# Regrouping a retention-and-adapters kernel so that two units share each TensorE array mode

## Chip, core and metric

The kernel runs on one core of a Trainium2 chip. The core has five engines that run side by side, each with its own queue of instructions in a fixed order: TensorE (PE in the profile; its weight loads are listed as PEld), VectorE (DVE), ScalarE (ACT), GpSimd (POOL) and SyncE (SP, which here only issues DMA transfers). They wait for each other through semaphores. TensorE writes only into PSUM, eight banks of 128 partitions by 2 KB; DVE and ACT read it from there. The metric is the time of one execution on the device in microseconds (us).

## What is computed

The first half is a retention layer: attention without softmax, with a causal mask that decays with the distance. The second half is a mixture of small low-rank adapters, of which each token uses its best two.

```python
# q, k, v: (B=8, H=8, S=576, D=64)
scores = q @ k.T / sqrt(D)
gamma  = 1 - 2.0 ** (-5 - arange(H))
Dmat   = where(i >= j, gamma ** (i - j), 0)
x      = (scores * Dmat) @ v              # then (B*S, H*D) = (4608, 512)

logits = x @ w_gate                       # 8 experts
topk   = two largest logits; w = softmax over these two
out    = x + sum over the two of  w * (x @ A[e]) @ B[e]     # rank 16
```

## The kernel before

**Tiling.** The 576 positions are four chunks of 128 and one of 64. A *quad* is one chunk of four batches (half of the eight), so there are ten quads; `quads` lists them, chunk by chunk. A *unit* is two batches of a quad: `units` has 16 full units (0 to 15) and two half units (16 and 17) for the last, 64 long chunk. Inside a chunk the products are computed directly with a mask; what comes from the earlier chunks is held in a decayed state `P`, one per pair of batches.

**Stages.** Each unit t passes these functions. The third column is the part of TensorE's array that its matmuls use, as the profile prints it (rows*columns): its *array mode*. The half units use 64*64 for S and R.

| stage | TensorE work | mode | what follows on other engines |
|---|---|---|---|
| `stage_T` | transposes q, k to `pqT`, `pkT` | 64*128 | copies to `qT`, `kT` by ACT (some by DVE) |
| `stage_S` | scores `ps` = kT . qT (half units: `pe`) | 64*128 | DVE multiplies by the mask into `rt` (`rh`) |
| `stage_Q` | `px` = state P . qT | 64*64 | nothing; no matmuls for units 0 to 3 |
| `stage_U` | `pu` = k . v, the state's update | 128*64 | DVE adds P into `pn`, POOL decays it into `P` |
| `stage_R` | `px` += v . rt | 128*64 | DVE scales it into `xT` |
| `stage_Z` | `pz` = xT . (A, gate) | 128*128 | DVE: `lg`, two largest, `ns` |
| `stage_V` | none | | ACT: two sigmoids `sg` |
| `stage_W` | none | | DVE: weights `cm`, weighted `zc`; frees `pz` |
| `stage_B` | transposes xT into `po` | 64*128 | nothing |
| `stage_X` | transposes zc into `pzt` | 128*128 | ACT copies it to `zT` |
| `stage_Y` | `po` += zT . B | 128*128 | ACT copies `po` to `osb` (half of it by DVE where `spread`), SP issues the output |

`scale_k` lets POOL multiply k by the decay in place, after k's transposition and before U.

**What sets the order.** The helpers `mm`, `vec` and `act` (lines 80 to 87) chain all instructions of TensorE, DVE and ACT in the order in which the stages are called, so the calls at the end of the kernel are the engines' queues. PSUM is handed out by `bank` and `done` (lines 102 to 110): `free` is a list, first in, first out; a bank that is given back goes to its end, and the next user waits for its last reader. The loads are issued by `issue(n)` for quad n + 2 when quad n begins; DMA issues stand on SP's queue, so one that waits for a free buffer holds the ones behind it, outputs too. The pool `io` holds three buffers each for q, k and v of a quad.

**The order before.** Unit 0 and 1 are written out by hand with the setup. Unit t in the steady part runs

```python
stage_S(t, (0,)); stage_V(t - 1); stage_T(t + 1, ("qT",))
stage_S(t, (1,)); stage_W(t - 1); stage_T(t + 1, ("kT",))
stage_B(t - 1); stage_Q(t); stage_U(t); scale_k(t + 1)
stage_R(t); stage_X(t - 1); stage_Z(t); stage_Y(t - 1)
```

so each unit's T is one unit ahead and its B, X, W and Y one unit behind. At unit 15, `stage_Q(16)` is called as well. The half units have an order of their own, and the last unit ends half by half (`gs`).

Of the kernel before, what the change touches and what calls it, by code (L numbers as in the profile page):

```python
# [10 lines left out]
FP32 = mybir.dt.float32  # L11
# [7 lines left out]
def kernel(  # L19
# [180 lines left out]
    def issue(n):  # L200
        if n >= len(quads):
            return
        c, qd = quads[n]
        first = n == 0
        tl = [
            iop.tile([128, QUAD, H, Dh], FP32, tag=tag, name=tag) for tag in ("q32", "k32", "v32")
        ]
        if c == NFULL:
            if qd > 0:
                return  # L210
            for src, dst in zip((q, k, v), tl):
# [40 lines left out]
    def is_full(t):  # L252
        return units[t][0] < NFULL
# [11 lines left out]
                op=ALU.mult,  # L265
            )

    def stage_T(t, names=("qT", "kT")):

        s = st.setdefault(t, {})  # L270
        for nm in names:
            src = nat[units[t]][0 if nm == "qT" else 1]
            dst = s[nm] = wk.tile([128, 2, HP, C], FP32, tag=nm, name=nm)
            ps = [bank([128, HP, 2, L], f"p{nm}") for _ in range(2)]
            for hp in range(HP):
                for b in range(2):
                    for g in range(2):
                        mm(
                            ps[g][:, hp, b, :],
                            lhsT=src[rows(g), b, 2 * hp : 2 * hp + 2, :],  # L280
                            rhs=id64[rows(g), :],
                            is_transpose=True,
                            start=True,
                            stop=True,
                        )
            for g in range(2):
                if is_full(t):
                    o = dst[:, :, :, rows(g)].rearrange("p b a i -> p a b i")
                else:
                    o = dst[:, g].rearrange("p a (b i) -> p a b i", b=2)  # L290
                if t < 2 and nm == "qT" or t < 3 and nm == "kT" and g == 1:
                    vec("tensor_copy", out=o, in_=ps[g])
                else:
                    act("copy", out=o, in_=ps[g])
            done(*ps)

    def stage_Q(t):
        c, qd, sl = units[t]
        s = st[t]
        s["px"] = px = [  # L300
            bank([128, HP, C], f"px{x}") for x in range(2)
        ]
# [94 lines left out]
    def stage_R(t):  # L397
# [5 lines left out]
        if is_full(t):  # L403
            for b in range(2):
                for hp in range(HP):
                    for ho in range(2):
# [9 lines left out]
                xt = mo.tile([128, HP, C], FP32, tag="xT", name="xT", bufs=6)  # L416
                vec("tensor_tensor", out=xt, in0=px[b], in1=asc[b], op=ALU.mult)
                s["xT"].append(xt)
            done(*px)
# [11 lines left out]
                            skip_group_check=True,  # L431
                        )
        for x in range(2):
            xt = mo.tile([128, HP, C], FP32, tag="xT", name="xT", bufs=6)
# [26 lines left out]

    BOTH = (0, 1)

    def stage_X(t, gs=BOTH):
        s = st[t]
        n = len(gs)
        pzt = bank([128, n, 128], "pzt", FP16)
        for y, g in enumerate(gs):
            mm(
                pzt[:, y, :], lhsT=s["zc"][g], rhs=ident16,  # L470
                is_transpose=True, start=True, stop=True,
            )
        zt = mo.tile([128, n, 128], FP16, tag=f"zT{n}", name="zT")
        act("copy", out=zt, in_=pzt)
        done(pzt)
        for y, g in enumerate(gs):
            s.setdefault("zT", {})[g] = zt[:, y, :]

    def stage_Z(t, gs=BOTH):
        s = st[t]  # L480
# [38 lines left out]
    def stage_W(t, gs=BOTH):  # L519
# [6 lines left out]
        zc = mo.tile([128, n, ER], FP16, tag=f"zc{n}", name="zc")  # L526
        for y in range(n):
            vec(
                "scalar_tensor_tensor",
# [78 lines left out]
    for t in range(NU):  # L608
        if units[t][2] == 0:
            issue(quads.index(units[t][:2]) + 2)  # L610
        if t == 0:
# [9 lines left out]
            for ho in range(2):  # L621
                gp.tensor_copy(out=AW[1][rows(ho)], in_=AW[0][rows(1 - ho)])
            gp.dma_start(out=Bcat, in_=moe_B.rearrange("e r d -> (e r) d"))
            stage_Q(0)
            stage_U(0)
            stage_R(0)
            stage_T(1, ("qT",))
            stage_T(1, ("kT",))
            scale_k(1)
            stage_Z(0)  # L630
            stage_S(1)
            stage_W(0)
            stage_Q(1)
            stage_U(1)
# [13 lines left out]
            continue  # L648
        if t == 1:
            continue  # L650
        if t == NU - 1:
            break
        if t == 2:
            stage_T(3, ("qT",))
            stage_B(1)
            stage_V(1)
            stage_S(2)
            stage_W(1)
            stage_T(3, ("kT",))
            stage_Q(2)  # L660
            stage_U(2)
            scale_k(3)
            stage_R(2)
            stage_X(1)
            stage_Z(2)
            stage_Y(1)
            continue
        if is_full(t):
            stage_S(t, (0,))
            stage_V(t - 1)  # L670
            stage_T(t + 1, ("qT",))
            stage_S(t, (1,))
            stage_W(t - 1)
            stage_T(t + 1, ("kT",))
            stage_B(t - 1)
            stage_Q(t)
            if not is_full(t + 1):
                stage_Q(t + 1)
            stage_U(t)
            scale_k(t + 1)  # L680
            stage_R(t)
            stage_X(t - 1)
            stage_Z(t)
            stage_Y(t - 1)
            continue

        stage_S(t)
        stage_W(t - 1)
        stage_T(t + 1)
        stage_B(t - 1)  # L690
        stage_R(t)
        stage_Q(t + 1)
        stage_X(t - 1)
        stage_Z(t)
        stage_W(t)
        stage_Y(t - 1)
        stage_S(t + 1)
        stage_B(t)
        stage_X(t)
        stage_R(t + 1)  # L700
        stage_Y(t)
        for g in range(2):
            stage_Z(t + 1, (g,))
            stage_W(t + 1, (g,))
        stage_B(t + 1)
        for g in range(2):
            stage_X(t + 1, (g,))
            stage_Y(t + 1, (g,), spread=True, last=True)
    return

# [1 line left out]
_INS = ['q', 'k', 'v', 'moe_w_gate', 'moe_A', 'moe_B']  # L712
_OUTS = [((4608, 512), 'float32')]
# [25 lines left out]
```

## Time and profile before

| what | value |
|---|---|
| median of 13 runs | 194.59 us (193.70 to 195.32) |
| the profiled execution's own time | 193.94 us |
| its span, first to last instruction | 192.1 us |
| TensorE's granted clock, mean | 0.992 of full speed |
| last po matmul's end, by the timeline | 187.56 us from the span's start |
| DMA | 38.73 MB, mean 202 GB/s |
| a masked product `rt` on DVE (128x512) | 0.686 us, x64 |
| a copy of `qT` or `kT` on ACT (128x512) | 0.590 us |
| k scaled on POOL (128x512) | 1.042 us, x32 |

A row of the timeline has the start and the time of a group in us, the engine, the line (81 for all matmuls, 84 for DVE, 87 for ACT: the helpers), the operation, "out<-in", the array mode for TensorE, the shape and the count. A bracket at its end is idle time of that engine just before, with what ended it. TensorE's matmuls overlap each other and their ends are modelled, so the distance from one start to the next says more than the printed time.

### The profile page before, as it was taken

The numbers are of one execution on the slowest core, as the hardware profiler recorded it, in microseconds if no ns is written. First come the engines' busy times: TensorE is split into PE (matmuls) and PEld (weight loads), VectorE is DVE, ScalarE is ACT, GpSimd is POOL, SyncE is SP. The second block draws the span as 40 slices with busy tenths as digits, with TensorE's granted clock in tenths as the row PEclk, the third lists the DMA queues.
The fourth block names the chain that finished last, engine by engine and source line by source line (L and its number), as shares of the span: only waits on it lengthen the run. The fifth ranks groups of instructions, "written<-read, shape, count | busy, mean of one in ns | idle before, by whom it ended". The sixth has DMA issues, their size and how long they took to land. (4 is left out here: it accounts for less than half of the span.)

```text
span 192.1 us, 8113 instructions
## 1 busy us (share of the span) xinstructions
PE 180.4 (94%) x3612; PEld 163.4 (85%) x3612; DVE 110.4 (57%) x281; ACT 72.0 (37%) x195; POOL 58.9 (31%) x70
## 2 busy tenths in 40 slices
PE   7899997999999999999999999999999999987870
PEld 2499997989999999999999999999999999986750
DVE  4467947574656564747465665646464645543650
ACT  4111163253526160707071615252525344160540
POOL 8994025040424242332414150606060510200000
PEclk9999999999999999999999999999999999999996
DMA  7999699998998999579799758998951102030343
GB/s 143 263 240 269 170 277 271 242 315 227 248 361 263 245 337 273 143 216 332 222 241 312 213 169 250 296 263 206 230 145 50 64 26 90 3 113 3 113 109 109
DMA packets 53746, 38.73 MB, mean 202 GB/s; under 512 B 27472, under 2 KB 49104, under 8 KB 53712
## 3 DMA queue, kind: packets, MB, share of 16 engines
q1 hardware_dynamic: 52736, 37.75, 70.1%
q8 instruction: 28, 0.46, 1.0%
q10 hardware_dynamic: 832, 0.34, 0.7%
q0 software_dynamic: 144, 0.13, 0.4%
q14 instruction: 6, 0.05, 0.1%
HBM read 28.91 MB, written 9.44 MB: 200 GB/s over the span
## 5 line engine op out<-in xcount | busy, mean ns | idle before, releaser
L261 POOL TENSOR_TENSOR k<-k,pack 128x512 f32<-128x512 f32 x32 | 32.7, 1042 | 79.9 <-PE pkT L81 69.3
L84 DVE TENSOR_TENSOR rt<-ps,mask 128x512 f32<-128x512 f32 x64 | 41.0, 686 | 16.5 <-PE ps L81 16.0
L81 PE MATMUL pz<-AW,xT 128*128 128x136 f32 x288 | 37.4, 283 | 0.2 <-DVE xT L84 0.2
L81 PE MATMUL ps<-qT,kT 64*128 64x128 f32 x512 | 35.7, 281 | 0.9 <-DVE kT L84 0.9
L81 PEld LDWEIGHTS pz<-AW,xT 128*128 128x128 f32 x288 | 34.6, 190 | 0.6 <-DVE xT L84 0.5
L81 PEld LDWEIGHTS ps<-qT,kT 64*128 64x128 f32 x512 | 31.0, 188 | 4.0 <-PE po L81 2.7
L87 ACT COPY osb<-po 128x256 f32<-128x256 f32 x68 | 20.6, 386 | 28.4 <-PE po L81 28.0
L81 PE MATMUL px<-rt,v 128*64 128x128 f32 x512 | 30.8, 273 | 0.0
L84 DVE TENSOR_TENSOR xT<-px,asc 128x512 f32<-128x512 f32 x36 | 24.6, 691 | 8.1 <-PE px L81 6.9
L81 PEld LDWEIGHTS px<-rt,v 128*64 128x64 f32 x512 | 27.8, 137 | 0.0
L87 ACT COPY zT<-pzt 128x256 f16<-128x256 f16 (+1 forms) x19 | 6.9, 361 | 53.4 <-PE pzt L81 53.4
L87 ACT COPY kT<-pkT 128x512 f32<-128x512 f32 x33 | 17.9, 590 | 14.2 <-PE pkT L81 14.2
L395 POOL TENSOR_TENSOR P<-pn,gdec 128x512 f32<-128x512 f32 x12 | 15.3, 1271 | 25.5 <-DVE pn L84 22.6
L87 ACT COPY qT<-pqT 128x512 f32<-128x512 f32 x32 | 17.2, 590 | 8.3 <-PE pqT L81 8.3
L81 PE MATMUL pu<-v,k 128*64 128x64 f32 x512 | 18.4, 225 | 1.6 <-POOL k L261 1.1
L81 PEld LDWEIGHTS pu<-v,k 128*64 128x64 f32 x512 | 16.3, 138 | 4.1 <-issue 2.6
L84 DVE COPY lg<-pz 128x16 f32<-128x16 f32 (+1 forms) x19 | 3.3, 173 | 26.6 <-PE pz L81 26.6
L84 DVE TENSOR_TENSOR pn<-pu,P 128x512 f32<-128x512 f32 x12 | 8.3, 692 | 16.0 <-PE pu L81 16.0
L81 PE MATMUL px<-qT,P 64*64 64x128 f32 (+1 forms) x512 | 15.9, 262 | 1.3 <-issue 1.3
L81 PEld LDWEIGHTS px<-qT,P 64*64 64x64 f32 x512 | 12.7, 133 | 2.3 <-issue 1.4
L81 PE MATMUL po<-id,xT 64*128 64x64 f32 x288 | 12.6, 224 | 0.7 <-DVE zc L84 0.7
L81 PE MATMUL pkT<-id,k 64*128 64x64 f32 x288 | 12.4, 223 | 0.1
(51 smaller groups left out, 150.0 us busy)
## 6 DMA issues: line engine op xcount, KB each, us to landing
out_dram<-osb SPq DMA_DIRECT2D x32, 256.0 KB, 3.8
q<-in_q_dram SPq DMA_DIRECT2D x4, 512.0 KB, 6.5
k<-in_k_dram SPq DMA_DIRECT2D x4, 512.0 KB, 6.8
v<-in_v_dram SPq DMA_DIRECT2D x4, 512.0 KB, 7.0
out_dram<-osb SPq DMA_DIRECT2D x6, 128.0 KB, 2.3
Arow<-in_moe_A_dram SPq DMA_DIRECT2D x1, 256.0 KB, 5.0
out_dram<-osb ACTq DMA_DIRECT2D x2, 128.0 KB, 2.7
Bcat<-in_moe_B_dram POOLq DMA_DIRECT2D x1, 128.0 KB, 4.9
```

The lines of the kernel that those rows point to most:

```text
L81: chain("pe", nc.tensor.matmul(*args, **kw))
L84: chain("dve", getattr(nc.vector, fn)(**kw))
L87: chain("act", getattr(nc.scalar, fn)(**kw))
L261: gp.tensor_tensor(out=kk[:, b], in0=kk[:, b], in1=gv[:, 0].unsqueeze(2).broadcast_to((128, H, Dh)), op=ALU.mult,)
L395: nc.gpsimd.tensor_tensor(out=Pt, in0=pn, in1=gdec, op=ALU.mult)
```

## The change

- *Order.* From unit 2 on, the two units of a quad go together through each mode. In the loop at an even t from 4 to 14, with u = t, t + 1: S of both, with the T of units t + 2 and t + 3 between their halves; B of units t - 4 and t - 3, one common X for both; Z of t - 2, Y of t - 4 and t - 3, Z of t - 1; Q of both; W of t - 2 and t - 1 (DVE alone); U and R of t, then of t + 1. So T runs a quad ahead, Z and W a quad behind, and B, X, Y two quads behind. The quad of units 4 and 5 has its own T at the end of the start and issues T of 6 and 7 at its end.
- *Start.* Units 2 and 3, T of 4 and 5 move into the part written out by hand; V(1) stands ahead of Y(0). U comes before Q in units 0 to 3, so that U gets the first bank of the free list. The copy of unit 0's kT is cut into one per batch (two on ACT, two on DVE).
- *Tail.* S(16) and Q(16) follow R(15), then the remaining stages of units 12 to 17.
- *Buffers.* q: two instead of three; qT: four instead of two; zc: four instead of three; zT: two instead of three; xT: eight instead of six. k, v and kT stay at three, three and two.

```diff
@@ issue
-            iop.tile([128, QUAD, H, Dh], FP32, tag=tag, name=tag) for tag in ("q32", "k32", "v32")
+            iop.tile([128, QUAD, H, Dh], FP32, tag=tag, name=tag, bufs=n)
+            for tag, n in (("q32", 2), ("k32", 3), ("v32", 3))
@@ stage_T
-    def stage_T(t, names=("qT", "kT")):
+    def stage_T(t, names=("qT", "kT"), shared=False):
-            dst = s[nm] = wk.tile([128, 2, HP, C], FP32, tag=nm, name=nm)
+            dst = s[nm] = wk.tile([128, 2, HP, C], FP32, tag=nm, name=nm, bufs=4 if nm == "qT" else 2)
...
-                if t < 2 and nm == "qT" or t < 3 and nm == "kT" and g == 1:
+                if t == 0 and nm == "kT":
+                    for b in range(2):
+                        x = dst[:, b, :, rows(g)]
+                        if g == 1:
+                            vec("tensor_copy", out=x, in_=ps[g][:, :, b])
+                        else:
+                            act("copy", out=x, in_=ps[g][:, :, b])
+                elif t < 2 and nm == "qT" or shared and g == 1:
                     vec("tensor_copy", out=o, in_=ps[g])
@@ stage_X
-    def stage_X(t, gs=BOTH):
-        n = len(gs)
+    def stage_X(ts, gs=BOTH):
+        todo = [(t, g) for t in ts for g in gs]
+        n = len(todo)
...
@@ the start (t == 0)
-            stage_Q(0)
             stage_U(0)
+            stage_Q(0)
...
-            stage_X(0)
+            stage_X([0])
             stage_Z(1)
+            stage_V(1)
             stage_Y(0, spread=True)
-            stage_T(2, ("kT",))
+            stage_T(2, ("kT",), shared=True)
+            stage_T(3)
             scale_k(2)
+            scale_k(3)
+            stage_S(2)
+            stage_W(1)
+            stage_S(3)
+            for u in (2, 3):
+                stage_U(u)
+                stage_Q(u)
+                stage_R(u)
+            for nm in ("kT", "qT"):
+                stage_T(4, (nm,), shared=True)
+            scale_k(4)
+            stage_T(5)
+            scale_k(5)
...
@@ the loop, in place of the two steady bodies
+        before, near = [u for u in (t - 4, t - 3) if u > 0], (t - 2, t - 1)
+        here = (t, t + 1)
+        for u in here:
+            for b, nm in enumerate(("qT", "kT")):
+                stage_S(u, (b,))
+                if t > 4:
+                    stage_T(u + 2, (nm,))
+            if t > 4:
+                scale_k(u + 2)
+        for u in before:
+            stage_B(u)
+        stage_X(before)
+        stage_Z(near[0])
+        stage_V(near[0])
+        for u in before:
+            stage_Y(u)
+        stage_Z(near[1])
+        stage_V(near[1])
+        if units[t][0] > 0:
+            for u in here:
+                stage_Q(u)
+        for u in near:
+            stage_W(u)
+        for u in here:
+            stage_U(u)
+            if units[t][0] == 0:
+                stage_Q(u)
+            stage_R(u)
+        if t == 4:
+            for nm in ("kT", "qT"):
+                stage_T(6, (nm,), shared=True)
+            scale_k(6)
+            stage_T(7)
+            scale_k(7)
@@ the tail, h = 16 and n = 17
+    stage_S(h); stage_Q(h); stage_B(h - 4); stage_B(h - 3); stage_X([h - 4, h - 3])
+    stage_Z(h - 2); stage_V(h - 2); stage_Y(h - 4, spread=True); stage_Y(h - 3, spread=True)
+    stage_W(h - 2); stage_R(h); stage_S(n); stage_Z(h - 1); stage_V(h - 1); stage_Q(n)
+    stage_W(h - 1); stage_B(h - 2); stage_B(h - 1); stage_X([h - 2, h - 1]); stage_Z(h)
+    stage_V(h); stage_Y(h - 2); stage_W(h); stage_R(n); stage_B(h); stage_Y(h - 1, spread=True)
+    stage_X([h]); stage_Z(n, (0,)); stage_V(n, (0,)); stage_Y(h, spread=True); stage_Z(n, (1,))
+    for g in range(2): stage_W(n, (g,))
+    stage_B(n)
+    for g in range(2): stage_X([n], (g,)); stage_Y(n, (g,), spread=True, last=True)
```

(The tail's calls stand on one line each in the source.)

More of the change, by code (lines that the diff above doesn't have):

```diff
@@ L299, in stage_Q @@
         s = st[t]
-        s["px"] = px = [
-            bank([128, HP, C], f"px{x}") for x in range(2)
-        ]
+        s["px"] = px = [bank([128, HP, C], f"px{x}") for x in range(2)]
         if c == 0:
@@ L415, in stage_R @@
                         )
-                xt = mo.tile([128, HP, C], FP32, tag="xT", name="xT", bufs=6)
+                xt = mo.tile([128, HP, C], FP32, tag="xT", name="xT", bufs=8)
                 vec("tensor_tensor", out=xt, in0=px[b], in1=asc[b], op=ALU.mult)
@@ L433, in stage_R @@
         for x in range(2):
-            xt = mo.tile([128, HP, C], FP32, tag="xT", name="xT", bufs=6)
+            xt = mo.tile([128, HP, C], FP32, tag="xT", name="xT", bufs=8)
             vec("tensor_tensor",
@@ L462 @@
     BOTH = (0, 1)
-    def stage_X(t, gs=BOTH):
-        s = st[t]
-        n = len(gs)
+    def stage_X(ts, gs=BOTH):
+        todo = [(t, g) for t in ts for g in gs]
+        n = len(todo)
         pzt = bank([128, n, 128], "pzt", FP16)
-        for y, g in enumerate(gs):
+        for y, (t, g) in enumerate(todo):
             mm(
-                pzt[:, y, :], lhsT=s["zc"][g], rhs=ident16,
+                pzt[:, y, :], lhsT=st[t]["zc"][g], rhs=ident16,
                 is_transpose=True, start=True, stop=True,
             )
-        zt = mo.tile([128, n, 128], FP16, tag=f"zT{n}", name="zT")
+        zt = mo.tile([128, n, 128], FP16, tag=f"zT{n}", name="zT", bufs=2)
         act("copy", out=zt, in_=pzt)
         done(pzt)
-        for y, g in enumerate(gs):
-            s.setdefault("zT", {})[g] = zt[:, y, :]
+        for y, (t, g) in enumerate(todo):
+            st[t].setdefault("zT", {})[g] = zt[:, y, :]
     def stage_Z(t, gs=BOTH):
@@ L525, in stage_W @@
         cm = mo.tile([128, n, E], FP32, tag=f"cm{n}", name="cm")
-        zc = mo.tile([128, n, ER], FP16, tag=f"zc{n}", name="zc")
+        zc = mo.tile([128, n, ER], FP16, tag=f"zc{n}", name="zc", bufs=4)
         for y in range(n):
@@ L623 @@
             gp.dma_start(out=Bcat, in_=moe_B.rearrange("e r d -> (e r) d"))
+            stage_U(0)
             stage_Q(0)
-            stage_U(0)
             stage_R(0)
             stage_T(1, ("qT",))
-            stage_T(1, ("kT",))
+            stage_T(1, ("kT",), shared=True)
             scale_k(1)
@@ L632 @@
             stage_W(0)
+            stage_U(1)
             stage_Q(1)
-            stage_U(1)
             stage_R(1)
@@ L648 @@
             continue
-        if t == 1:
+        if t < 4 or units[t][2] or not is_full(t):
             continue
[L651 to L708, printed above, removed]
@@ L709 @@
-    return
+        before, near = [u for u in (t - 4, t - 3) if u > 0], (t - 2, t - 1)
[14 more added lines that the diff above has]
+            stage_Y(u)
@@ new lines @@
+        stage_Z(near[1])
[16 more added lines that the diff above has]
+            scale_k(7)
+    h, n = NU - 2, NU - 1
@@ new lines @@
+    stage_S(h)
+    stage_Q(h)
+    stage_B(h - 4)
+    stage_B(h - 3)
+    stage_X([h - 4, h - 3])
+    stage_Z(h - 2)
+    stage_V(h - 2)
+    stage_Y(h - 4, spread=True)
+    stage_Y(h - 3, spread=True)
+    stage_W(h - 2)
+    stage_R(h)
+    stage_S(n)
+    stage_Z(h - 1)
+    stage_V(h - 1)
+    stage_Q(n)
+    stage_W(h - 1)
+    stage_B(h - 2)
+    stage_B(h - 1)
+    stage_X([h - 2, h - 1])
+    stage_Z(h)
+    stage_V(h)
+    stage_Y(h - 2)
+    stage_W(h)
+    stage_R(n)
+    stage_B(h)
@@ L712 @@
+    stage_Y(h - 1, spread=True)
+    stage_X([h])
+    stage_Z(n, (0,))
+    stage_V(n, (0,))
+    stage_Y(h, spread=True)
+    stage_Z(n, (1,))
+    for g in range(2):
+        stage_W(n, (g,))
+    stage_B(n)
+    for g in range(2):
+        stage_X([n], (g,))
+        stage_Y(n, (g,), spread=True, last=True)
 _INS = ['q', 'k', 'v', 'moe_w_gate', 'moe_A', 'moe_B']
```

## The prediction, made before the changed kernel was run

> **What bounds the kernel now.** I read the page's part 1 first, then the list of waits, then the timeline of TensorE (PE), then that of VectorE (DVE) and ScalarE (ACT) at the places that PE's gaps point to. The page's busy shares:
>
> ```profile
> PE 180.4 (94%) x3612; PEld 163.4 (85%) x3612; DVE 110.4 (57%) x281; ACT 72.0 (37%) x195; POOL 58.9 (31%) x70
> ```
>
> PE is busy 94% of the span and nobody else comes near, so I looked at what PE does with its time. One unit of the steady part, PE's timeline (start, time, group):
>
> ```profile
> 66.98 1.16 PE L81 MATMUL ps<-qT,kT 64*128 64x128 f32 x16
> 67.98 0.66 PE L81 MATMUL pqT<-id,q 64*128 64x64 f32 x16
> 68.47 1.12 PE L81 MATMUL ps<-qT,kT 64*128 64x128 f32 x16
> 69.42 0.66 PE L81 MATMUL pkT<-id,k 64*128 64x64 f32 x16
> 69.91 0.67 PE L81 MATMUL po<-id,xT 64*128 64x64 f32 x16
> 70.51 1.10 PE L81 MATMUL px<-qT,P 64*64 64x128 f32 x32
> 71.54 1.15 PE L81 MATMUL pu<-v,k 128*64 128x64 f32 x32
> 72.53 1.92 PE L81 MATMUL px<-rt,v 128*64 128x128 f32 x32
> 74.38 0.29 PE L81 MATMUL pzt<-ident,zc 128*128 128x128 f16 x2
> 74.50 2.07 PE L81 MATMUL pz<-AW,xT 128*128 128x136 f32 x16
> 76.41 0.60 PE L81 MATMUL po<-Bcat,zT 128*128 128x256 f16 x4
> 76.94 1.16 PE L81 MATMUL ps<-qT,kT 64*128 64x128 f32 x16
> ```
>
> No row has an idle bracket, and the unit repeats after 76.94 - 66.98 = 9.96 us. The starts are what to read (ends are modelled). The column such as 64*128 is the part of the array a matmul uses: its mode. A unit crosses four modes: 64*128 (S, T, B), 64*64 (Q), 128*64 (U, R), 128*128 (X, Z, Y). Compare pkT with the po that follows: same shape, same count, but pkT takes 0.49 us to the next start (69.42 to 69.91) and po, which is followed by another mode, 0.60. So a crossing costs PE time although no row calls it idle.
>
> The places where PE does stand still are at the two ends:
>
> ```profile
> 32.22 1.15 PE L81 MATMUL pu<-v,k 128*64 128x64 f32 x32 [1.13 <-POOL k L261]
> 41.68 1.15 PE L81 MATMUL pu<-v,k 128*64 128x64 f32 x32 [0.47 <-DVE cm L84]
> 171.00 0.71 PE L81 MATMUL po<-id,xT 64*128 64x64 f32 x15 [0.39 <-DVE zc L84]
> 174.91 0.34 PE L81 MATMUL px<-qT,P 64*64 64x64 f32 x7 [1.26 <-issue]
> ```
>
> The first is put down to POOL, but DVE's timeline has the four rt products of S(2) from 29.63 to 32.11, and PE starts 0.1 later: a PSUM bank that the last product frees. The second and third likewise wait for banks that DVE's W frees. The fourth, inside a run of equal matmuls with no semaphore, I take for waiting for code (a reading).
>
> **Part 1: the steady order (units 4 to 15).** No matmul is added or removed; they are regrouped so that a quad crosses four modes once instead of twice. The price of a crossing, from the single records' starts at the unit above, as excess over the spacing inside each group: Y to S 0.203 instead of 0.109, then 0.213 instead of 0.112: 0.195. B to Q 0.152 instead of 0.057, then 0.160 instead of 0.109: 0.146. Q to U 0.199 instead of 0.089, then 0.106 instead of 0.058: 0.158. R to X 0.205 instead of 0.102: 0.103. Sum 0.60 per unit, 1.20 per quad. The new crossings are R to S, B to X, Z to Q, Q to U. The first and third do not occur in the steady part before; each consists of a leaving half (0.09 to 0.11) and an entering half (0 to 0.10), so between 0.09 and 0.21; with 0.15 each, four cost 0.60. S straight after a transposition starts 0.05 late even inside one mode (68.47 to the second pair 0.165 instead of 0.112); there are three such places per quad where there were two. Gain per quad 1.20 - 0.60 - 0.05 = 0.55 us. Five quads (6 to 15) give 2.75. The quad of units 4 and 5 has no transpositions between its S and gains 0.65. Together **3.4 us**.
>
> [...]
>
> [...] In the new 64*128 run PE makes, per half S and one T, 0.95 + 0.49 = 1.44 us of work; DVE must multiply two ps banks by the mask:
>
> ```profile
> 68.17 1.29 DVE L84 TENSOR_TENSOR rt<-ps,mask 128x512 f32<-128x512 f32 x2 [0.88 <-PE ps L81]
> 69.61 1.29 DVE L84 TENSOR_TENSOR rt<-ps,mask 128x512 f32<-128x512 f32 x2
> ```
>
> 1.29 against 1.44, and ACT 2 x 0.54 for the T. Banks go round in order, so a half S reuses the bank of two halves earlier, 2.9 us before. DVE enters with one xT product left over (0.69) and ends some 0.3 us before PE wants the last of these banks for Z. X, Z, Y then find W of the quad before long done; U's bank was a po that ACT empties (4 x 0.3 per unit) over 1 us earlier. The xT (8), zc (4) and qT (4) buffers just cover the longer life; kT (2) is free since T(t+2) stands behind S(t). I cost all of this at nothing; if the cover goes, it costs per quad what DVE is late.
>
> **Part 2: the start.** Splitting kT's copy in two and giving U bank 5 (released by the first product) instead of bank 7 (by the third) moves PE's start at 8.98 forward by about 0.27 (DVE's 0.69 copy becomes a 0.42 one, the osb row) and U(0) by up to 0.12. But T(1) wants the second half of k, which landed at 15.4, and PE was there at 15.53: nearly all is given back. I take 0.1, ends 0 and 0.4. From 26.75 on the new order puts S(3) ahead of U(2): the stalls of 1.13 and 0.47 go (v of quad 1 landed by 30.7, POOL's k of unit 2 is done at 29.5: in time for a U(2) at 33), and four crossings (0.6) go: 2.2 us. Against it: V(1)'s two sigmoids (0.51) now stand in ACT's queue ahead of the osb copies and of kT(2), so S(2) comes at 29.05, not 28.47 (0.6); S(3) waits for ACT's kT(3) (0.3); DVE takes eight rt, W(1), two P and four xT in a row and reaches its share of kT(4), qT(4) 0.8 after PE is ready for S(4), and 0.2 at S(6). T(8) needs k of quad 4: q, k, v of quad 4 now stand on SP's queue ahead of the Y(1) outputs, behind v of quad 3 (issued at 47.48 to 50.98); at 0.27 MB/us k lands near 62.8, PE wants it at 62.6: 0 to 1.5, I take 0.3. Sum against 2.2. The q ring of two buffers holds SP until T(n-2) is done, but SP reached q of quad 2 only at 25.5 for lack of DMA room, ten us after T(1). **Start: 0, ends -1.5 and +1.5.** Later a quad has 19.4 us for 4 MB (206 GB/s; the page's slices carry 215 to 330 when loaded): no wait.
>
> **Part 3: the tail.** From R(15)'s end PE's old path took 187.56 - 165.22 = 22.34 us. The new order has 4.8 us of PE work more behind R(15) (Q(16) 1.25, Z(14) 1.9, three B 1.5, X and Y of 12 and 13 1.1, less T(17) 1.0): 27.1 to compare with. The new tail, added up: S, Q, R of 16 and 17 6.3; six B 3.0; X 0.6; four Z 7.6; Y of 12 to 16 2.2; thirteen crossings 2.0; X(14,15) waiting for zc(15), behind the xT and rh products in DVE's queue, 0.6; after Z(17) the chain lg, sg, zc, zT, po with B(17) beside it 2.6. Sum 24.9, a gain of 2.2: the stalls 0.39, 1.26, 0.28 and 0.23 find other work. The code wait I do not believe gone: R(16), S(17) are again 128 matmuls and their loads within 2 us. With one of 1.3, **tail 0.9**, ends -1.5 and 2.2 (no code wait; or three). Output issues on SP (0.33 to 0.59 each, eight in the last 7 us) stay beside it.
>
> **Sum.** 3.4 + 0 + 0.9 = 4.3, less 0.1 for what meets at SP's end. The profiled execution took 193.94 (span 192.1): 189.7. It lies 0.65 under the median of 194.59; so 190.4.
>
> **Rivals.**
> (a) *Regained PE time is eaten by new waits at both ends*: code fetching bites at S(16)-Q(16), R(16)-S(17) and Q(17), and DVE's and DMA's lateness at units 4 to 8 reaches its bad end. 3.4 - 1.5 - 0.6 = 1.3: 193.3. For it: the start and end are all new orders. Against: both ends bad at once.
> (b) *DVE paces the 64*128 run*: the margin of 0.3 us per run is small. If a masked product beside two POOL scalings in a row takes 0.78 instead of 0.645, eight are 1.08 longer, PE waits 0.8 at Z in each quad and, with the gain of 0.55, the steady part gets slower from there on; at 0.85 (1.6 - 0.3 = 1.3 a quad, six quads 8 against 4.2 gained) the time is 198. Against: the second row of the pair above ran partly beside POOL's k (70.10 to 72.14) at the same 1.29.
> (c) *No code wait, start clean*: 188.5; part of the main case's spread.
> That the change does not do what it says can be left out: the instruction order shows four crossings per quad.
>
> **How the numbers follow.** Main case (188.5 to 192) 0.63, at 190.4; (a) 0.22; (b) 0.09; the rest (c beyond, no change) 0.06. What a measurement of this kernel can tell from no change is about 0.2%, 0.4 us. Faster 0.87 (main, c and nearly all of a), same 0.03, slower 0.10. Range 188.2 to 193.5.
>
> **What would show it.** Right: from unit 6 on PE's timeline repeats after 19.35 to 19.45 us per quad, with four mode changes and no idle bracket; the pu row at 32 has none. Wrong: idle brackets `<-DVE` at pz or ps in every quad (b); a bracket at pkT of unit 8 over 1.5 us; brackets `issue` in the half units (a).

## The result and the profile after

| what | before | after |
|---|---|---|
| median | 194.68 us (193.49 to 196.22, 48 runs) | 191.51 us (189.02 to 192.29, 11 runs) |
| ratio, 95% interval | | 0.9779 (0.9751 to 0.9808) |
| the profiled execution's own time | 193.94 us | 189.61 us |
| its span | 192.1 us | 187.9 us |
| last po matmul's end | 187.56 us | 183.20 us |

The kernel is faster by 2.2% in the ratio, 1.9 to 2.5% by its interval: clear of noise, not clear of 2%. The ratio leaves out executions more than 1.5% above the fastest, here four of the eleven after, all at a granted clock of 0.970 to 0.982; with every execution counted the medians give 0.984, and the runs below tie the low clock to the change itself. The page's busy shares after:

```profile
PE 176.2 (94%) x3612; PEld 163.5 (87%) x3612; DVE 114.6 (61%) x294; ACT 65.9 (35%) x177; POOL 58.7 (31%) x70
```

The same 3612 matmuls take 176.2 us instead of 180.4, and PE is still the engine that bounds. One quad of the steady part, PE's timeline of after (start, time, group):

```profile
140.27 1.16 PE L81 MATMUL ps<-qT,kT 64*128 64x128 f32 x16
...
145.58 0.66 PE L81 MATMUL pkT<-id,k 64*128 64x64 f32 x16
146.08 1.17 PE L81 MATMUL po<-id,xT 64*128 64x64 f32 x32
147.19 0.40 PE L81 MATMUL pzt<-ident,zc 128*128 128x128 f16 x4
147.42 2.07 PE L81 MATMUL pz<-AW,xT 128*128 128x136 f32 x16
149.33 1.04 PE L81 MATMUL po<-Bcat,zT 128*128 128x256 f16 x8
150.20 2.02 PE L81 MATMUL pz<-AW,xT 128*128 128x136 f32 x16
152.15 1.98 PE L81 MATMUL px<-qT,P 64*64 64x128 f32 x64
154.06 1.15 PE L81 MATMUL pu<-v,k 128*64 128x64 f32 x32
155.04 1.92 PE L81 MATMUL px<-rt,v 128*64 128x128 f32 x32
156.79 1.10 PE L81 MATMUL pu<-v,k 128*64 128x64 f32 x32
157.72 1.92 PE L81 MATMUL px<-rt,v 128*64 128x128 f32 x32
159.57 1.16 PE L81 MATMUL pe<-qT,kT 64*64 64x64 f32 x64
```

Read the mode column from top to bottom: it changes four times in the quad, and no row has a bracket. The first half unit's S follows 159.57 - 140.27 = 19.30 us after the quad's first, against two units of 9.96 before. At the start the stall of 1.13 us at pu is gone:

```profile
33.16 1.15 PE L81 MATMUL pu<-v,k 128*64 128x64 f32 x32
```

But there is something that was not there before. PE's timeline of after from the first S of unit 6 to that of unit 8, with the T of unit 8 in between:

```profile
59.27 1.16 PE L81 MATMUL ps<-qT,kT 64*128 64x128 f32 x16
61.05 0.71 PE L81 MATMUL pqT<-id,q 64*128 64x64 f32 x16 [0.62 <-DMA q<-in_q_dram]
61.58 1.14 PE L81 MATMUL ps<-qT,kT 64*128 64x128 f32 x16
64.98 0.72 PE L81 MATMUL pkT<-id,k 64*128 64x64 f32 x16 [2.27 <-DMA k<-in_k_dram]
...
81.90 1.16 PE L81 MATMUL ps<-qT,kT 64*128 64x128 f32 x16
```

Twice within 4 us PE waits for a load of quad 4, 2.89 us in the brackets. By the starts the quad loses more: 81.90 - 59.27 = 22.63 us, 3.3 above 19.30. This is the largest stand-still of the new kernel. Where the 4.36 us between the two last po ends come from, each term from the two timelines:

| stretch | measured in the traces | predicted |
|---|---|---|
| steady quads: 5 x (19.91 - 19.30), less a stand-still of about 0.47 in the quad of units 10 and 11 | +2.6 | +2.75 |
| from R(15)'s end to the last po: 27.1 (the old path with the same work) - 23.6 | +3.5 | +0.9 |
| waits for q and k of quad 4 at unit 8, by the starts | -3.3 | -0.3 |
| the rest of the start, with the quad of units 4 and 5 (what is left over) | +1.6 | about +0.95 |
| sum | +4.4 | +4.3 |

(19.91 is the mean over the old steady part; 23.6 is 183.2 - 159.57.) The sum agrees, but two of its terms are off by 2.6 and 3.0 us, in opposite directions. The gain of the tail is not all the new order's: 1.26 us of the old tail were a stand-still that a second profile of before, shown below, has at half the length. And the median lies 1.9 us above the profiled execution, where before it lay 0.7 above. So the questions for the runs are: what the crossings are really worth, what the DMA wait costs and why it comes, and what spreads the executions from 189.0 to 192.3.

### The profile page after: what moved, and what is told of

It reads as the page before. It is cut to its first block, busy times and chain, and to the rows that moved or that the text cites. A ratio compares the mean times of both kernels' runs of the same rounds, so it can differ in the third digit from the quotient of the medians.

```text
span 187.9 us, 8116 instructions
## 1 busy us (share of the span) xinstructions
PE 176.2 (94%) x3612; PEld 163.5 (87%) x3612; DVE 114.6 (61%) x294; ACT 65.9 (35%) x177; POOL 58.7 (31%) x70
## 5 line engine op out<-in xcount | busy, mean ns | idle before, releaser
L401 POOL TENSOR_TENSOR P<-pn,gdec 128x512 f32<-128x512 f32 x12 | 15.3, 1277 | 65.4 <-DVE pn L84 62.6
L81 PE MATMUL ps<-qT,kT 64*128 64x128 f32 x512 | 34.6, 279 | 0.7 <-DVE kT L84 0.6
L87 ACT COPY qT<-pqT 128x512 f32<-128x512 f32 x30 | 16.1, 592 | 38.0 <-PE pqT L81 38.0
L87 ACT COPY kT<-pkT 128x512 f32<-128x512 f32 (+1 forms) x32 | 17.1, 583 | 30.7 <-PE pkT L81 19.5
L87 ACT ACTIVATE sg<-lg,ns 128x8 f32<-128x8 f32 x36 | 9.0, 294 | 26.5 <-DVE ns L84 26.2
L87 ACT COPY osb<-po 128x256 f32<-128x256 f32 x60 | 17.4, 385 | 1.7 <-PE po L81 1.0
L81 PEld LDWEIGHTS pkT<-id,k 64*128 64x128 f32 x288 | 11.1, 139 | 4.1 <-issue 3.1
L81 PE MATMUL px<-qT,P 64*64 64x128 f32 (+1 forms) x512 | 14.1, 259 | 0.0
```

Of the source, the lines that this page charges most:

```text
L81: chain("pe", nc.tensor.matmul(*args, **kw))
L87: chain("act", getattr(nc.scalar, fn)(**kw))
L401: nc.gpsimd.tensor_tensor(out=Pt, in0=pn, in1=gdec, op=ALU.mult)
```

## The experiments

Each run is compared with the kernel before on the same chip. Runs in one group below shared a chip. The clock given beside a time is TensorE's mean granted clock in that execution.

### First group: the waits at unit 8, and the price of a crossing

**The changed kernel again**, as the measure for this group.

> The changed kernel once more, for a second profile and a second set of times. Its first eleven times fell in two groups, 189.0 to 190.0 us and 191.3 to 192.3 us. Theory D (DMA): PE stands at pkT of unit 8 for k of quad 4 (2.27 us in the first profile), and how late k is differs from execution to execution; then the wait at that row in this profile, with the profiled execution's own time, lies on the line 189.6 us at 2.3 us of wait: each us of wait more is a us of time more. Theory C (clock): the waits are the same, but the granted clock differs by one stretch of about 3.4 us at half speed; then the wait is 2.3 again and a slower execution shows it in the granted clock.

Measured: median 191.56 us (190.18 to 192.49), ratio 0.9801 (0.9754 to 0.9848). The trace shows what the first one did not. PE's timeline of this run at the same place:

```profile
64.10 0.83 PE L81 MATMUL pkT<-id,k 64*128 64x64 f32 x16 [1.80 <-DMA k<-in_k_dram]
64.77 1.84 PE L81 MATMUL ps<-qT,kT 64*128 64x128 f32 x16
66.40 1.06 PE L81 MATMUL pqT<-id,q 64*128 64x64 f32 x16
67.25 1.65 PE L81 MATMUL ps<-qT,kT 64*128 64x128 f32 x16
68.74 0.66 PE L81 MATMUL pkT<-id,k 64*128 64x64 f32 x16
```

The ps after the wait takes 1.63 us to the next start instead of 1.00, the next 1.49 instead of 0.94: the same matmuls, slower. The view by windows says why. Its columns are the stretch, its length, then the busy time and number of instructions of PE, weight loads, DVE, ACT and POOL, then the granted clock, the DMA share and GB/s. This run:

```profile
61.00:64.00 3.00, 1.30 (x28) 1.10 (x23) 2.44 (x4) 1.39 (x3) 1.32 (x2) 1.00 1.05 283
64.00:66.00 2.00, 1.90 (x30) 1.89 (x32) 0.00 (x0) 0.99 (x2) 0.99 (x1) 0.74 1.00 288
66.00:68.00 2.00, 2.00 (x29) 2.00 (x28) 1.29 (x2) 0.59 (x3) 1.05 (x2) 0.50 1.11 364
68.00:70.00 2.00, 2.00 (x54) 2.00 (x54) 1.07 (x2) 0.76 (x3) 0.58 (x1) 0.91 0.77 185
```

After the stand-still the granted clock is 0.50 in one stretch, 64.95 to 68.36 in the clock records, that is 3.41 us. From pkT's start to the end of the quad this run takes 82.71 - 64.10 = 18.61 us; the first profile of after, in which the clock stayed at 1.00, took 81.90 - 64.98 = 16.92. So the half clock costs 1.69 us, half of the stretch, on top of the wait that precedes it. The wait is thus worth more than its bracket, in those executions where it is followed by such a stretch. Neither theory holds as it was put: the wait is shorter than in the first profile and the time longer (190.18 against 189.61 us), so it is not on theory D's line; the half clock of theory C is there, but the waits are not the same.

**v of quad 3 behind q and k of quad 4.** Nobody wants v of quad 3 before U(6); q and k of quad 4 are wanted earlier.

```diff
@@ issue
+        elif (c, qd) == quads[3]:
+            load(0, 0, 4)
+            load(1, 0, 4)
+            late.append(load)
+        elif (c, qd) == quads[4]:
+            load(0, 0, 4)
+            load(1, 0, 4)
+            late.pop()(2, 0, 4)
+            load(2, 0, 4)
```

> v of quad 3 is issued behind q and k of quad 4, nothing else. Both q and k of quad 4 should land one load (3.8 us) earlier, before PE asks for them. Theory D: the waits of 0.62 us (q) and 2.27 us (k) at unit 8 go, the profiled time falls by 2.9 us to about 186.7 us, and the two groups of times close to one. Theory C: the time falls by the 2.9 us, but the two groups, 2 us apart, remain. Rival (DMA has no room at all in the first 80 us): the wait moves to k of quad 5 or to v and the time falls by under 1 us.

Measured: median 187.29 us (186.02 to 188.54), ratio 0.9575 (0.953 to 0.962), 4.3 us under the changed kernel beside it. The profile fell on its longest time, 188.54 us; even there PE's timeline has at unit 8 only

```profile
64.43 0.71 PE L81 MATMUL pkT<-id,k 64*128 64x64 f32 x16 [0.28 <-DMA k<-in_k_dram]
```

and no q wait; this profile has waits for k of 0.42 us at unit 1 and of 1.07 at T(4) instead. Every one of its executions has a clock of 0.988 or more, against 0.979 to 0.991 in the group's first run. So one reordered megabyte gives back the wait and the half clock together. In this group's profile of the changed kernel the two cost 82.71 - 59.70 - 19.30 = 3.7 us from the first S of unit 6 to that of unit 8; the medians differ by 4.3, with a spread of over 2 us in each run. That the lateness of the DMA was the price of the new order is shown.

**The opposite: v of quad 4 ahead of its k**, which makes k one transfer later.

```diff
@@ issue
+        elif (c, qd) == quads[4]:
+            for n in (0, 2, 1):
+                load(n, 0, 4)
```

> v of quad 4 is issued ahead of k of quad 4, so that k lands one load (3.7 us) later than in the changed kernel. Theory D: PE's wait at pkT of unit 8 grows from 2.3 to about 6 us and the time by 3.7 us, to about 193.3 us in the profile. If the long stand-still also lowers TensorE's granted clock, 1 to 2 us come on top. Rival (what k waits for is not the place in the queue): the time stays.

Measured: median 195.94 us (195.34 to 198.65), ratio 1.0039 (1.0002 to 1.0076): the whole gain is gone. PE's timeline of this run, then a window for PE alone (stretch, length, PE's busy time and number, granted clock, DMA share, GB/s):

```profile
71.66 1.12 PE L81 MATMUL pkT<-id,k 64*128 64x64 f32 x16 [6.21 <-DMA k<-in_k_dram]
```

```profile
69.00:73.00 4.00, 1.34 (x20) 0.52 0.97 309
```

The bracket grew from 1.80 to 6.21 us, 4.4 more, and the medians differ by 4.4. That the two agree so well is in part chance: this profile took 197.74 us, with waits of 0.77 and 2.25 us for q and k at unit 1 and a first half-clock stretch behind them, from 18.00 to 21.41. At unit 8 the half clock holds for two such stretches, 6.83 us from 69.20 on; but the first of them lies partly over idle time, so it costs PE little more than one, 1.95 us: from pkT to the quad's end 90.53 - 71.66 = 18.87, against 16.92. All ten executions of this kernel have a mean clock of 0.962 to 0.979.

**Q, U and R of one unit, then of the other.** This gives back the pairing in one place: two crossings more per quad, no other work changed.

```diff
@@ the loop
-        if units[t][0] > 0:
-            for u in here:
-                stage_Q(u)
-        for u in near:
-            stage_W(u)
-        for u in here:
+        for i, u in enumerate(here):
+            stage_Q(u)
+            if i == 0:
+                for w in near:
+                    stage_W(w)
             stage_U(u)
-            if units[t][0] == 0:
-                stage_Q(u)
             stage_R(u)
```

> In each quad of units 4 to 15 Q, U, R of one unit are followed by Q, U, R of the other: two crossings of array modes more per quad (R to Q, Q to U), all other work and its order on the other engines as in the changed kernel, W included. Theory M (a crossing costs PE 0.10 to 0.20 us): 6 quads x 2 x 0.15 = 1.8 us slower, and PE's timeline repeats after 19.6 to 19.7 us per quad instead of 19.3. Rival (the crossings are free and the gain came from the two ends): no change within 0.4 us.

Measured: median 192.67 us (191.73 to 193.83), ratio 0.9873 (0.9829 to 0.9916), 1.1 us above the changed kernel; the two intervals overlap a little, so the trace must decide. PE's timeline of this run:

```profile
96.22 1.10 PE L81 MATMUL px<-qT,P 64*64 64x128 f32 x32
97.25 1.15 PE L81 MATMUL pu<-v,k 128*64 128x64 f32 x32
98.23 1.92 PE L81 MATMUL px<-rt,v 128*64 128x128 f32 x32
100.08 1.10 PE L81 MATMUL px<-qT,P 64*64 64x128 f32 x32
101.12 1.15 PE L81 MATMUL pu<-v,k 128*64 128x64 f32 x32
102.10 1.92 PE L81 MATMUL px<-rt,v 128*64 128x128 f32 x32
```

64*64 appears twice per quad. The first S of the quads are at 84.34, 103.95, 123.55 and 143.16. So they repeat after 19.60 us instead of 19.30: two crossings cost 0.30, so 0.15 each. That is the value taken in the prediction.

### Second group: the small parts, and idle matmuls

**The split copy and the order of U and Q undone.**

```diff
@@ stage_T
-                if t == 0 and nm == "kT":
-                    for b in range(2):
...
-                elif t < 2 and nm == "qT" or shared and g == 1:
+                if t < 2 and nm == "qT" or (shared or t == 0 and nm == "kT") and g == 1:
@@ the start
-            stage_U(0)
             stage_Q(0)
+            stage_U(0)
```

> The changed kernel with unit 0's kT copied whole again and Q before U in unit 0. Theory (my step on the start): the 0.27 us that the split copy gains at the first ps row are given back where T(1) waits for the second half of k, so the time is the changed kernel's within 0.3 us, and the pkT row of unit 1 shows no wait for DMA. Rival: the edits are worth their 0.3 to 0.4 us to the end, and this kernel is slower by that.

Measured: median 189.71 us (188.02 to 193.04), ratio 0.9731 (0.968 to 0.9783). Alone this would say that the edit costs time; but the executions run from 188.02 at a clock of 0.994 to 193.04 at 0.982, a spread of 5 us, far more than the edit could be worth, and the changed kernel was not on this chip. As expected, the pkT row of unit 1 has no wait for DMA. See its second run below.

**Eight idle matmuls ahead of unit 8's kT**, in the time in which PE would wait: PE has something to do until the load is nearly there, and the wait itself is not shortened.

```diff
@@ the loop, T of unit 8
+                if u == 6 and nm == "kT":
+                    fill = bank([128, 512], "fill")
+                    for _ in range(8):
+                        mm(fill, lhsT=idle[:, 0:128], rhs=idle, start=True, stop=True)
+                    done(fill)
```

> The changed kernel with eight idle fp16 matmuls (0.216 us each in the start of every profile, 1.73 us together) put on PE ahead of unit 8's pkT, where it waits 1.8 to 2.3 us for k of quad 4. They do no useful work. Theory C2 (the stand-still itself costs a stretch of half clock in part of the executions): PE does not stand still for long any more, no stretch of half speed follows, the times close to one group near the changed kernel's fast ones, 190.0 us, median lower by up to 1.5 us although work was added. Rival D2 (only the lateness of k counts): the median stays or rises by up to 0.5 us, and the spread of the times stays 2 us.

Measured: median 188.57 us (187.95 to 193.80), ratio 0.971 (0.9676 to 0.9743). The clock is 0.99 or more in all executions but the 193.80 one (0.988, so a half-clock stretch does not explain that one), and in this profile pkT has no DMA bracket, since PE is busy when the load lands. What this does to the time is weighed with its second run.

**Loads reordered further, and W ahead of B in the tail.** The first edit together with k before q in quad 2 (for the wait at T(4)), and W of the last unit's first half ahead of Y(16) on DVE's queue, instead of behind it.

```diff
@@ issue (with v of quad 3 behind q and k of quad 4, as above)
+        elif (c, qd) == quads[2]:
+            for x in (1, 0, 2):
+                load(x, 0, 4)
@@ the tail
-    stage_V(n, (0,))
+    stage_W(n, (0,))
...
-    for g in range(2):
-        stage_W(n, (g,))
+    stage_W(n, (1,))
```

(`stage_W` calls `stage_V` itself where that has not been done.)

> The changed kernel with v of quad 3 behind q and k of quad 4 (as in e1), k of quad 2 ahead of q of quad 2, and the last unit's first W ahead of unit 16's output copies. Theory D: the waits for DMA at units 4 and 8 and 0.4 us of PE's wait for zc at the end go: 0.3 to 1.3 us under e1, 186.0 to 187.0 us in the median. Rival: k of quad 2 was late because DMA was, and q of quad 2 is now the one waited for: as e1.

Measured: median 186.11 us (185.33 to 187.46), ratio 0.9579 (0.9544 to 0.9615), the same as with the first edit alone (0.9575), as the rival said, though q of quad 2 is not waited for. The profile took 187.46 us, the longest of its six times: the wait at T(4) is gone, but PE waits 1.16 us for k at unit 8. The tail did not get shorter: from the last Z to the last po it takes 3.3 us against 3.1, with two waits of PE for zT (1.02 and 0.36) in place of three (0.48 for zc, 0.36 and 0.51 for zT). So this edit of the tail is of no use.

**The kernel before, once more**, for a second trace of its tail.

> The kernel before, unchanged, for a second profile of it. Theory F (the idle 1.26 us inside the run of px matmuls of unit 17 is a wait for instructions that comes in every execution): the same bracket `issue` at the same place, 1.2 to 1.4 us. Rival: it is chance, and this profile has none there or has one elsewhere.

Measured: 194.68 us. PE's timeline of this run at the stand-still which the first profile put down to `issue` with 1.26 us:

```profile
175.71 0.34 PE L81 MATMUL px<-qT,P 64*64 64x64 f32 x7 [0.62 <-issue]
```

The place is the same, the length is half, and two more brackets of this kind, 0.24 and 0.70 us, appear in the steady part. So a stand-still of this kind is not a fixed cost: it varies from one execution to the next. That it is a wait for code is the author's reading; no run shows it.

### Third group: second runs on a third chip

**The changed kernel.**

> The changed kernel on the same chip as the three runs beside it, since two chips of the earlier runs differ by more than 1 us. It is the baseline for them. Theory C2: of its executions those with a granted clock of 0.982 or less are about 2 us slower than those at 0.987 or more.

Measured: median 189.62 us (188.91 to 192.21), ratio 0.9759 (0.9708 to 0.9809). Four executions at clocks of 0.988 to 0.99 took 188.91 to 189.83; two at 0.979 and 0.981 took 191.48 and 192.21. The profile, one of the four, has waits of 1.01 us (k at unit 1) and 1.45 us (k at unit 8).

**The split copy undone, again.**

> The start edits of unit 0 undone, now beside the changed kernel on one chip. Step on the start: within 0.5 us of the changed kernel's median. Rival: slower by more than that, since the 0.3 us reach the end.

Measured: median 190.33 us (189.87 to 192.42), ratio 0.9802 (0.9755 to 0.9849). All six executions have a clock between 0.980 and 0.982. Its profile shows a k wait of 1.74 us and a half-clock stretch of 3.41 us behind it. The median is 0.7 us above the changed kernel's beside it, more than the 0.5 expected, but only two of the six executions of that kernel have so low a clock. So the medians do not tell what the split copy is worth. The traces narrow it down at its place: T(4) starts at 38.51 to 38.77 us in six profiles with the edit, at 38.76 and 38.90 in two without, and at 39.31 in one with the edit and a late k at unit 1. That is 0.2 us or so, and only where this load is in time.

**The idle matmuls, again.**

> The eight idle matmuls ahead of unit 8's pkT, beside the changed kernel on one chip. Theory C2: no execution has a granted clock under 0.987, and the median lies 0.5 to 2 us under the changed kernel's. Rival D2: equal medians within 0.5 us or slower, and low clocks in some executions as before.

Measured: median 189.24 us (188.31 to 192.55), ratio 0.9709 (0.9664 to 0.9754). Here q of quad 4 was late as well, by 1.50 us, and k by another 0.25 after the idle matmuls. In time the run is 0.4 us under the changed kernel beside it, inside the spread: inconclusive. The clock speaks more clearly, if the kernel with the split undone is counted too, which has the same wait at unit 8: on these two chips one of twelve executions with the idle matmuls has a clock below 0.985 (0.982, against the expectation that none would), of the eighteen without them ten. Of the changed kernel alone on this chip it is two of six. So the idle matmuls probably keep the clock up; they leave the wait itself.

**The loads reordered, the tail as in the changed kernel**, and unit 0's outputs issued behind v of quad 3, so that no output stands ahead of these loads.

```diff
@@ issue (with k before q in quad 2, as above)
+        elif (c, qd) == quads[3]:
+            load(0, 0, 4)
+            load(1, 0, 4)
+            late.insert(0, load)
+        elif (c, qd) == quads[4]:
+            load(0, 0, 4)
+            load(1, 0, 4)
+            late.pop(0)(2, 0, 4)
+            for f in late:
+                f()
+            load(2, 0, 4)
@@ stage_Y
-                nc.sync.dma_start(out=out[n0 : n0 + C, :], in_=of[:, g, :])
+                o, i = out[n0 : n0 + C, :], of[:, g, :]
+                if t == 0:
+                    late.append(lambda o=o, i=i: nc.sync.dma_start(out=o, in_=i))
+                else:
+                    nc.sync.dma_start(out=o, in_=i)
```

> As e1 (v of quad 3 behind q and k of quad 4), with k of quad 2 ahead of q of quad 2 and with unit 0's outputs issued behind v of quad 3; the end as in the changed kernel. k of quad 4 lands another 2 us earlier than in e1. Theory D: no wait for DMA is left at unit 8, every execution's clock is 0.987 or more, and the time is 3.5 to 5 us under the changed kernel's median, 0.954 to 0.960 of the kernel before. Rival: the wait moves to T of units 6 or 10 and the time is the one of e1 or above.

Measured: median 185.66 us (185.12 to 186.90), ratio 0.9553 (0.9513 to 0.9592): the lowest of all, though its interval overlaps those of the other two versions with reordered loads, 4.0 us under the changed kernel on the same chip and 8.9 under the kernel before. The page's busy shares, then PE's timeline of this run at unit 8:

```profile
PE 175.8 (96%) x3612; PEld 163.5 (89%) x3612; DVE 114.6 (62%) x294; ACT 66.0 (36%) x177; POOL 58.8 (32%) x70
```

```profile
60.74 1.14 PE L81 MATMUL ps<-qT,kT 64*128 64x128 f32 x16
61.69 0.69 PE L81 MATMUL pkT<-id,k 64*128 64x64 f32 x16
62.19 1.14 PE L81 MATMUL ps<-qT,kT 64*128 64x128 f32 x16
```

As theory D has it, pkT follows ps after 0.95 us with no bracket, as in any later quad. PE's busy time is that of the changed kernel (175.8 against 176.2); only its idle time is gone. Its six executions lie within 1.8 us, at clocks of 0.988 to 0.995.

## Why the prediction was right, point by point

**Part 1, the steady order: right.** The prediction has 19.35 to 19.45 us per quad, the trace 19.30; 0.55 gained per quad against 0.61. The prices of the crossings, read from the starts of single records, carried it, and the run with two more crossings gives 0.15 for each, which was only an estimate for the new ones.

**That DVE holds the pace in the 64*128 run (rival b): fell.** No pz or ps row of a steady quad has a bracket `<-DVE`. The margin worked out from the masked products, 1.29 us for two against 1.44 of PE's work, was enough; after has the pair at 1.29 too.

**Part 2, the start: mechanism right, one term mis-sized.** The stalls of 1.13 and 0.47 us went as described. From 38 to 60 us PE's timeline has no bracket, so the waits of 0.8 and 0.2 assumed at S(4) and S(6) were not there, and PE came to unit 8 earlier than expected. The step that is off is the load: "T(8) needs k of quad 4 ... at 0.27 MB/us k lands near 62.8, PE wants it at 62.6: 0 to 1.5, I take 0.3". It was right that this is where the next wait would be, and why; but the waits cost 3.3 us in the first profile, and the brackets for k alone are 1.80 and 1.45 in the two further profiles of the same kernel. The rate is one thing that was wrong. In before the step from 10 to 15 MB takes from 41.5 to 59.8 us, 0.27 MB/us; after, from 41.4 to 61.5, 0.25. In SP's timeline of after each of these loads of 1 MB holds the queue for 3.2 to 3.8 us:

```profile
48.00 3.24 SPq L225 DMA_DIRECT2D v<-in_v_dram  x1
51.70 3.77 SPq L225 DMA_DIRECT2D q<-in_q_dram  x1
55.92 3.43 SPq L225 DMA_DIRECT2D k<-in_k_dram  x1
```

The same 15 MB are 1.7 us later. Why the rate is lower stays open. Before had outputs among these loads and after has none, but that does not settle it: two versions with reordered loads, too, have loads alone in such a stretch, and move 0.24 MB/us (the first, 44.2 to 58.1 us) and 0.27 (the last, 40.4 to 56.0). In the end k let PE go at 64.98, 2.1 us behind the forecast of its landing (62.8), and PE without its two waits would have been there at 61.7 (2.43 us behind the quad's first S, as from 81.90 to 84.33 in the next quad), 0.9 before the 62.6 expected: together the 3.0 us of the table. The sign named for it beforehand, a bracket over 1.5 us at unit 8's pkT, came.

**Split copy and U first: right.** "Nearly all is given back, I take 0.1": the idle bracket ahead of the first ps became 0.64 us instead of 0.91, and pkT of unit 1, at 16.10, waits for its k with a bracket of 0.27 in the same profile.

**Part 3, the tail: mechanism right, the assumed stand-still did not come.** The walk through the tail gave 24.9 us and a gain of 2.2, from which 1.3 was taken for one stand-still of the kind `issue`. Measured is 23.6 and no such row in the half units, in the profile of after or in the ten other profiles of that order of the tail. The gain is 3.5: the 2.2 of the walk, from which nothing had to be taken, and 1.3 from its steps. Of these the 0.6 us wait for zc(15) did not come (no bracket in the half units before 181.26), the last chain took 3.1 instead of 2.6, and the other 1.2 are in matmuls and crossings that were added up too high. The stand-still of this kind that after does show lies elsewhere, in the steady part:

```profile
108.19 0.46 PE L81 MATMUL po<-id,xT 64*128 64x64 f32 x8 [0.26 <-issue]
```

The steady quads without such a row take 19.30 us, this one 19.77: the 0.47 us of the table.

**Rival (a), regained time eaten at both ends: half of it came.** The DMA wait at unit 8 is its bad end, and at 3.3 us reached beyond the 1.5 that the prediction allowed for it; the `issue` brackets at the other end did not come.

**What was missing: the clock.** The prediction has 189.7 for the profiled execution, measured 189.61; and 190.4 for the median, by the distance of 0.65 that the kernel before has between the two, measured 191.51. That distance does not carry over, since after a stand-still at unit 8 some executions lose the clock for 3.41 us and 1.7 us of time, others not. One such stretch takes 3.41 x 0.5 / 188 = 0.009 off the mean clock, which shows in the list of executions. Of the changed kernel's 24 listed ones the 15 with a mean clock below 0.985 have a median of 191.65 us, the other nine of 189.61. The kernel before has none in the 39 listed with the runs above, the three versions with reordered loads none in 18. The half clock is seen in the second profile of the changed kernel and in two of its variants; that each of the 15 has it at unit 8 is inferred from the mean. Not every long time is explained so: one of the nine took 192.49 us at a clock of 0.987.

So the predicted time came out near because the steady gain was as worked out, and because a tail 2.6 us better and a load wait 3.0 us worse nearly cancel. That they cancel is luck. What the loads cost can be had back: the version with reordered loads keeps both gains.

## What to carry to other kernels

Where matmuls in different array modes alternate, price each change of mode from the starts of single records (0.10 to 0.20 us here), and group by mode; but a grouping that moves work a whole tile group forward moves the deadline of its loads forward too, so put the loads in the order in which the new schedule wants them. Allow for a spread in the transfer rate when working out such a deadline (0.24 to 0.27 MB/us in these versions), and look at what comes after a stand-still of TensorE, not only at its bracket (about 1.7 us from the half clock here). When the spread of the executions grows with a change, list the granted clock of each before explaining their median.

## What the runs showed of the hardware

*Half clock after a short stand-still.* Stand-stills of 1.74 us (the split copy undone, third group) and 1.80 us (the changed kernel, first group) at pkT were each followed by one stretch of 3.41 us at a granted clock of 0.50, which cost about 1.7 us. A stand-still of 2.27 us (with 0.62 shortly before) was not. In the clock records of a profile the changes of the clock lie whole multiples of 3.41 us apart, wherever PE stood still (18.00, 21.41, 69.20 and 76.02 us with v ahead of k: 1, 14 and 2 intervals; 6.06 and 183.55 us in the first profile of after: 52). Laid on this grid, the stand-stills of 1.74 and 1.80 us lie whole in one interval each, while the boundary at 64.08 splits that of 2.27. PE alone in two such intervals of the first profile of after, then of the second (stretch, length, PE's busy time and number, granted clock, DMA share, GB/s):

```profile
60.67:64.08 3.41, 1.66 (x32) 1.00 0.97 288
64.08:67.50 3.42, 2.52 (x58) 1.00 0.98 272
```

```profile
61.54:64.95 3.41, 1.61 (x34) 1.00 1.01 253
64.95:68.36 3.41, 3.41 (x42) 0.50 1.08 357
```

Within one interval in mid-kernel, idle times of up to 1.67 us (the run with two crossings more) and of 1.75 (the first pair) were not followed by half clock; 1.74, 1.80 (the second pair), and 2.70, 3.41 and 2.46 (v ahead of k) were. So in these profiles the half clock follows an interval of which PE idles about half or more, and the longer gap of 2.27 us, which a boundary splits into 1.37 and 0.90, is not followed by it. The ends of matmuls are modelled, so 1.74 and 1.75 cannot be told apart, and no run moved the gap on purpose.

*Idle matmuls in the wait* left one of 12 executions below a clock of 0.985, against 10 of 18 without them on the same two chips. Their effect on the time is below what these runs resolve.

*Stand-stills without a releaser move.* 1.26 and 0.62 us at the same place in two profiles of one kernel, none in the half units of the new order, and brackets of 0.24 to 0.70 us at other places from profile to profile. Their cause stays open.
